# Chunked attention, soft mixture of experts and a softplus MLP on one core: where the 1 MB expert loads stand in SyncE's load queue

## The chip, the cores and the metric

The kernel runs on one core of one Trainium2 chip. The metric is device time in microseconds for one execution; lower is better. All weights and inputs lie in HBM when the kernel starts, and every load is issued by SyncE (SP) on one hardware DMA queue.

## What is computed

Attention is done in chunks of 64 rows inside each head, its output becomes the token matrix x (4608 x 512), a soft mixture of experts turns x into another 4608 x 512 matrix, and an MLP with softplus follows:

```python
scores = scale * np.matmul(q_c, k_c.transpose(0, 1, 2, 4, 3))   # 8 x 8 heads, 9 chunks of 64
attn = softmax(scores); out = np.matmul(attn, v_c)
x = out.transpose(0, 2, 1, 3).reshape(4608, 512)
logits = x @ phi                                  # 32 slots, 8 experts with 4 each
slot_input = softmax(logits, axis=0).T @ x
h = np.maximum(slot_input[e] @ w1[e], 0.0)        # w1: 8 x 512 x 1024
slot_out[e] = h @ w2[e]                           # w2: 8 x 1024 x 512
x = softmax(logits, axis=1) @ slot_out
g = softplus(x @ w_in); out = g @ w_out           # 512 -> 2048 -> 512
```

All of it is float32. w1 and w2 are 16 MiB each.

## The kernel before

The work has three stages on the engines' streams.

**Attention** goes through 36 units, each two heads by 512 tokens. The steps of a unit u are `lq` (loads q and k, 256 KB each, line 265, or 261 for the first four units), `lv` (loads v for two units, line 272), `A0`/`A1` (TensorE transposes of q and k, line 406), `S` (scores, line 437), `C` (transposes of the probabilities, line 470), `D` (times v, line 489), `E` (transposes of x, line 524), and every fourth unit `F` and its followers (the router's logits, lines 542 to 614). q and k have three buffers each, `raw`; unit u+3 can be loaded once `A1` of unit u has run.

**The experts.** The w1 weights come in sixteen loads of 1 MiB, and so do the w2 weights (`load`, lines 285 to 307; a load into a slot w0 to w7 is issued as two DMAs of 512 KB). The list `W1` names the SBUF slot of each w1 load, `W2` that of each w2 load. Slots w, g and i lie beside attention's buffers; the five slots d0 to d4 (loads 5 to 9 of w1) lie in attention's own space. A step `close` gives up attention's buffers piece by piece: d0 needs all `A1`, d1 and d2 need all `S`, d3 and d4 need all `D`. Once attention is done, `H` number n multiplies the slot inputs by w1 load n (line 933, eight matmuls each), and `SO` number n multiplies the hidden values by w2 load n (line 975, sixteen matmuls each). Loads 5 to 15 of w2 go into slots that an `H` or `SO` has to have read before: load 5 (slot w0) follows `H` 0, load 6 follows `H` 1. Beside `SO` runs the chain `c1` to `c6`, `d`, `dc` (lines 795 to 858): the token's softmax over slots, in three groups, each ending in a GpSimd step `c6` (line 845) and three times four TensorE transposes `d` (line 852) into cT. Before `SO` 14 and `SO` 15 stand four and three pairs of filling matmuls (line 916, table `FILL`).

**The MLP** follows: 72 steps of matmuls (lines 1086, 1144, 1146, 1148) with softplus on VectorE, ScalarE and GpSimd.

The order on every engine is made when the program is built: `issue` (lines 74 to 136) is a list scheduler. It takes the steps with their costs (table `COST`, in microseconds), buffers and ranks, simulates one clock for each engine, and at every turn issues the step that can start first, by rank where several can. A step with `after` isn't issued before the steps named there. What it picks is the order in each engine's stream; on the chip each engine goes through its stream in that order. A `lw` step (a 1 MiB load) has a rank of 100 or more, an `lq` step the rank of its unit, so a `lw` step goes between two `lq` steps only where the simulated SP would otherwise stand idle.

Of the kernel before, what the change touches and what calls it, by code (L numbers as in the profile page):

```python
# [17 lines left out]
LAG = 3  # L18
BUSY = 36
WAIT = 0  # L20
FILL = {("SO", 14): 4, ("SO", 15): 3, ("o", 0): 2}


# [8 lines left out]


COST = {
# [110 lines left out]
def kernel(  # L145
# [56 lines left out]
    def open_pool(nm):  # L202
        c = ExitStack()
        pools[nm] = c.enter_context(tc.tile_pool(
            name="slots_" + nm, bufs=1, side="right", reuse_waits="tile"))
        pool_ctx.append(c)
# [411 lines left out]
    by = {}  # L618

    def add(nm, key, fn, deps=(), take=(), give=(), rank=0.0, cost=None, after=()):  # L620
        s = Step(nm, key, fn, [by[d] for d in deps if d in by], take, give, rank, cost,
                 [by[d] for d in after])
        by[nm, key] = s
        steps.append(s)

    for u in range(NU):
# [4 lines left out]
            cost={"SP": 2.4} if G == MIXED else None)  # L631
# [27 lines left out]
        n = HP - 1 if G == NG - 1 else 0  # L659
# [61 lines left out]
    def at(f, *a):  # L721
        return lambda e, held: f(*a)

    for n, sl in enumerate(W1):
        if sl[0] != "d":
            add("lw", ("w1", n), at(load, "w1", n, sl), rank=100 + n)
    for n in range(5):
        add("lw", ("w2", n), at(load, "w2", n, W2[n]), rank=130 + n)
    ends = ((raw_ctx, "A1", ["d0"]), (qk_ctx, "S", ["d1", "d2"]), (v_ctx, "D", ["d3", "d4"]))
    deps = []  # L730
    for i, (c, nm, sls) in enumerate(ends):
        add("close", i, at(lambda c, sls: (c.close(), [open_pool(sl) for sl in sls]), c, sls),
            deps + [(nm, k) for k in range(NU)])
        deps = [("close", i)]
        for sl in sls:
            n = W1.index(sl)
            add("lw", ("w1", n), at(load, "w1", n, sl), deps, rank=110 + n)

    def warm_up(x, n):
        p = tr_tile(0)  # L740
# [11 lines left out]
    for a in range(4):  # L752
        sl = slice(32 * a, 32 * a + 32)
# [3 lines left out]
    for a in range(4):  # L757
        sl = slice(32 * a, 32 * a + 32)
# [155 lines left out]
    def fill(key, t):  # L914
        for _ in range(FILL.get(key, 0)):
            nc.tensor.matmul(
                out=t[:, 0:256], lhsT=ident, rhs=acc[:, 0:256], start=True, stop=True)
# [277 lines left out]
    for nm, n in AFTER:  # L1195
        r += 1
        if nm == "wi":
            for pr in range(2):
                sl = WI[n][0][pr]
# [3 lines left out]
        else:  # L1203
            sl = W2[n] if nm == "w2" else f"w{n}"
# [74 lines left out]
    for c in range(4):  # L1279
# [4 lines left out]
        n, d = need[c]  # L1284
# [21 lines left out]
    for n in range(NQ):  # L1306
        t, qd = order[n]
        ps = pieces.get(n, [(0, 4)])
        b, j = divmod(t // 2, 3)
# [62 lines left out]
    for s in steps:  # L1372
# [12 lines left out]
        if s.nm in ("cb0", "cx0") and s.key[:2] == ("wi", 1):  # L1385
            s.after = [*s.after, by["mx", (WAIT, 0)]]

# [31 lines left out]
```

## Time and profile before

| | |
|---|---|
| Median of 3 runs | 681.0 us (674.77 to 687.27) |
| The profiled execution | 677.68 us |
| its span on the core | 675.9 us |
| mean granted TensorE clock, share of full speed | 0.982 |
| TensorE matmuls busy | 636.2 us (94%) |
| moved by DMA | 107.93 MB |

The profile is that of one execution. The span runs from the first to the last instruction; the profiled execution's own time is 1.8 us longer. Times in the trace count from the start of the span. Attention ends at about 171 us, `H` runs from 174 to 188, `SO` from 192 to 224, and the MLP takes the rest.

### The profile page before, as it was taken

What the parts mean: (1) busy time and instruction counts of PE and PEld (TensorE: products, weight loads), DVE (VectorE), ACT (ScalarE), POOL (GpSimd) and SP (SyncE); (2) the same over time, 40 slices, a digit from 0 to 9 for tenths busy, and PEclk for the clock granted to TensorE, in tenths of its full rate; (3) what the DMA queues carried; (4) which work ended last, traced back from release to release, by engine and by line L of the source; (5) the groups of instructions that cost most, each with busy time, mean ns of one, the idle gap of its engine ahead of it and who ended that gap; (6) DMA issues with size and microseconds to landing.
All of it is one profiled execution on the core that took longest, in us unless ns stands there. A gap on an engine that the chain in (4) does not pass through costs nothing.

```text
span 675.9 us, 14115 instructions
## 1 busy us (share of the span) xinstructions
PE 636.2 (94%) x5849; PEld 511.0 (76%) x5849; DVE 428.0 (63%) x630; ACT 335.0 (50%) x511; POOL 237.9 (35%) x205
## 2 busy tenths in 40 slices
PE   5899889988987899999999999999999999999997
PEld 4688777766354677788788788888888888888885
DVE  1678777775337699879887867754555554545551
ACT  2575556553136699734655955544333333333330
POOL 4233233220214446513222234444433344443341
PEclk7999999999997999999999999999999999999999
DMA  9799879899999803112313410222414222231412
GB/s 176 194 253 267 247 216 289 225 322 419 413 409 410 357 32 112 44 64 93 125 64 123 189 63 31 82 75 79 110 62 126 63 86 101 78 110 64 120 36 62
DMA packets 80543, 107.93 MB, mean 160 GB/s; under 512 B 42464, under 2 KB 60896, under 8 KB 78560
## 3 DMA queue, kind: packets, MB, share of 16 engines
q1 hardware_dynamic: 80480, 107.04, 48.9%
q8 instruction: 46, 0.75, 0.4%
q14 instruction: 17, 0.14, 0.1%
HBM read 88.15 MB, written 18.87 MB: 158 GB/s over the span
## 4 chain that ended last, share of the span: by engine, by line
PE 83%; DVE 7%; ACT 3%; issue 3%; POOL 1%; DMA 1%; SPq 1%; POOLq 0%; DVEq 0%; ACTq 0%
PE trm L1148 18%; PE trm L1146 18%; PE trm L1144 18%; PE ph L1086 5%; PE tr L406 4%; PE X L489 3%; PE S L437 2%; PE tr L470 2%; PE tr L524 2%; PE hps L933 2%; PE sops L975 2%; PE tr L542 2%; PE tr L600 1%; DMA q<-in_q_dram 1%; DVE nm L448 1%
## 5 line engine op out<-in xcount | busy, mean ns | idle before, releaser
L1125 POOL TENSOR_TENSOR g<-hTm,g 128x1024 fp32r<-128x1024 f32 (+1 forms) x37 | 87.3, 2359 | 105.2 <-ACT g L1121 101.4
L1111 ACT ACTIVATE hTm<-hTm 128x1024 f32<-128x1024 f32 (+2 forms) x51 | 51.5, 1011 | 77.6 <-DVE hTm L1105 77.3
L1105 DVE TENSOR_SCALAR hTm<-ph 128x1024 uint32<-128x1024 uint32 (+2 forms) x51 | 59.0, 1157 | 35.8 <-PE ph L1086 35.8
L423 POOL COPY T<-T 64x512 f32<-64x512 f32 x72 | 43.9, 610 | 102.5 <-ACT T L415 101.7
L1115 DVE SCALAR_TENSOR_TENSOR hTm<-ph,hTm 128x1024 f32<-128x1024 f32 (+1 forms) x37 | 44.2, 1194 | 24.8 <-ACT hTm L1111 24.7
L1121 ACT CAST g<-hTm 128x1024 fp32r<-128x1024 f32 (+1 forms) x37 | 38.0, 1026 | 39.6 <-DVE hTm L1115 39.6
L1160 DVE TENSOR_TENSOR i<-trm,i 128x512 f32<-128x512 f32 x52 | 35.7, 686 | 31.6 <-PE trm L1148 31.4
L415 ACT COPY T<-tr 128x512 f32<-128x512 f32 x72 | 40.9, 588 | 25.3 <-PE tr L406 25.2
L1086 PEld LDWEIGHTS ph<-cT,Tc 128*128 128x128 f32 x288 | 43.6, 190 | 11.6 <-issue 3.1
L1086 PE MATMUL ph<-cT,Tc 128*128 128x256 f32 x288 | 47.1, 286 | 2.1 <-DVE ph L1115 1.7
L1105 DVE TENSOR_SCALAR siT<-ph 128x1024 uint32<-128x1024 uint32 (+1 forms) x25 | 29.5, 1180 | 25.8 <-PE ph L1086 25.8
L1111 ACT ACTIVATE siT<-siT 128x1024 f32<-128x1024 f32 (+1 forms) x25 | 25.7, 1028 | 36.9 <-DVE siT L1105 36.9
L1125 POOL TENSOR_TENSOR g<-siT,g 128x1024 fp32r<-128x1024 f32 x12 | 28.9, 2404 | 42.5 <-ACT g L1121 42.5
L1125 DVE TENSOR_TENSOR g<-ph,g 128x1024 fp32r<-128x1024 f32 (+2 forms) x27 | 29.8, 1102 | 11.1 <-ACT g L1121 11.1
L448 DVE TENSOR_REDUCE nm<-S 128x8 f32<-128x512 f32 x36 | 24.7, 687 | 16.7 <-PE S L437 16.6
L1121 ACT CAST g<-ph 128x1024 fp32r<-128x1024 f32 (+2 forms) x27 | 24.9, 921 | 20.6 <-DVE ph L1115 17.0
L406 PE MATMUL tr<-ident,q 128*128 128x128 f32 x144 | 29.1, 285 | 6.1 <-DMA q<-in_q_dram 5.0
L437 PE MATMUL S<-T 64*64 64x64 f32 x1152 | 24.9, 223 | 7.1 <-DVE P L454 2.5
L437 PEld LDWEIGHTS S<-T 64*64 64x64 f32 x1152 | 20.7, 135 | 14.4 <-issue 10.0
L406 PE MATMUL tr<-ident,k 128*128 128x128 f32 x144 | 28.6, 280 | 1.2 <-issue 1.1
L462 ACT ACTIVATE P<-P 128x512 f32<-128x512 f32 x36 | 22.9, 638 | 11.6 <-DVE P L454 11.6
L454 DVE TENSOR_TENSOR P<-S,nm 128x512 f32<-128x512 f32 x36 | 24.5, 680 | 2.1 <-PE S L437 1.3
(457 smaller groups left out, 1770.5 us busy)
## 6 DMA issues: line engine op xcount, KB each, us to landing
part<-i SPq DMA_DIRECT2D x18, 512.0 KB, 2.6
i<-part SPq DMA_DIRECT2D x18, 512.0 KB, 3.6
q<-in_q_dram SPq DMA_DIRECT2D x32, 256.0 KB, 4.2
k<-in_k_dram SPq DMA_DIRECT2D x32, 256.0 KB, 4.6
vbm<-in_v_dram SPq DMA_DIRECT2D x40, 128.0 KB, 4.3
g<-in_moe_w_dram SPq DMA_DIRECT2D x5, 1024.0 KB, 7.9
d<-in_moe_w_dram SPq DMA_DIRECT2D x5, 1024.0 KB, 12.3
i<-in_moe_w_dram SPq DMA_DIRECT2D x5, 1024.0 KB, 15.6
```

The source lines that it names most:

```text
L406: nc.tensor.transpose(c, t[:, h, 2 * rr:2 * rr + 2, :].rearrange("p r d -> p (r d)"), ident)
L423: nc.gpsimd.tensor_copy(out=t[a:a + 64, :, 1], in_=t[b:b + 64, :, 2 * h])
L437: nc.tensor.matmul(out=sp[64 * o:64 * o + 64, b, 64 * i:64 * i + 64], lhsT=cs[:, 0], rhs=cs[:, 1], start=True, stop=True)
L1086: nc.tensor.matmul(out=ph(n, a, b)[:, j - a, :], lhsT=K["Tc"][:, f * 128:(f + 1) * 128], rhs=K["cT"][:, t * TT:(t + 1) * TT], start=True, ...
L1105: nc.vector.tensor_scalar(out=scratch(n, a, b).bitcast(U32), in0=ph(n, a, b).bitcast(U32), scalar1=0x80000000, scalar2=None, op0=ALU.bitwi ...
L1111: nc.scalar.activation(out=y, in_=y, func=AF.Softplus)
L1115: nc.vector.scalar_tensor_tensor(out=soft(n, a, b), in0=ph(n, a, b), scalar=0.0, in1=y, op0=ALU.max, op1=ALU.add)
L1121: nc.scalar.copy(out=V["gs", n][:, 0, a:b], in_=soft(n, a, b))
L1125: tt(e)(out=s[:, 1, a:b], in0=soft(n, a, b), in1=s[:, 0, a:b].bitcast(F32), op=ALU.subtract)
L1144: nc.tensor.matmul(out=po, lhsT=s[:, 0, j, ts_], rhs=wr[:, hs], start=(n in begin and j == 0), stop=False)
L1146: nc.tensor.matmul(out=po, lhsT=s[:, 0, j, ts_], rhs=wr[:, ls], start=False, stop=False)
L1148: nc.tensor.matmul(out=po, lhsT=s[:, 1, j, ts_], rhs=wr[:, hs], start=False, stop=(j == 3 and n in finish))
```

## The change

A new table `PARK` gives seven of the w1 loads a rank that is the number of a unit, instead of 100 and more, and ties each with `after`: load n comes behind the `lq` step before unit PARK[n] and ahead of that of unit PARK[n]. The costs of `lq`, `lv` and of these loads in the scheduler's table are set lower. The five loads into d0 to d4 get a rank of 140 and more and depend on the first five w2 loads.

```diff
+PARK = {0: 9, 1: 14, 2: 18, 3: 22, 4: 26, 10: 30, 11: 33}
 FILL = {("SO", 14): 4, ("SO", 15): 3, ("o", 0): 2}
...
-    "lq": {"SP": 1.7}, "lv": {"SP": 2.7}, "lwi": {"SP": 1.35},
+    "lq": {"SP": 1.55}, "lv": {"SP": 2.45}, "lwi": {"SP": 1.35},
...
     for n, sl in enumerate(W1):
         if sl[0] != "d":
-            add("lw", ("w1", n), at(load, "w1", n, sl), rank=100 + n)
+            add("lw", ("w1", n), at(load, "w1", n, sl), rank=PARK.get(n, 100 + n),
+                cost={"SP": 2.35} if n in PARK else None)
+            if n in PARK:
+                by["lq", PARK[n]].after = [by["lw", ("w1", n)]]
+                by["lw", ("w1", n)].after = [by["lq", PARK[n] - 1]]
...
         for sl in sls:
             n = W1.index(sl)
-            add("lw", ("w1", n), at(load, "w1", n, sl), deps, rank=110 + n)
+            add("lw", ("w1", n), at(load, "w1", n, sl), deps + [
+                ("lw", ("w2", j)) for j in range(5)], rank=140 + n)
```

On SP's queue, five 1 MiB loads stand between attention's q, k and v loads before (slots w0, w1, g0, g1, g2), and nine now: w0, w1, w4, g0, g1, g2, w5, w2, w3 (w4 and w5 have no entry in the table; the scheduler finds them a place). The end of attention's loads reads, before:

```order
L272 DMA vbm_115<-in_v_dram 128x4x64 x4
L265 DMA q_2682<-in_q_dram 128x2x256
L265 DMA k_2683<-in_k_dram 128x2x256
L265 DMA q_2741<-in_q_dram 128x2x256
L265 DMA k_2742<-in_k_dram 128x2x256
L304 DMA g2_2789<-in_moe_w1_dram 128x2048
L265 DMA q_2834<-in_q_dram 128x2x256
L265 DMA k_2835<-in_k_dram 128x2x256
L272 DMA vb2_116<-in_v_dram 128x4x64 x4
```

and with the change, the same stretch of SP's queue, from the 1 MiB load in slot w2 on:

```order
L300 DMA w2a_2440<-in_moe_w1_dram 128x1024
L300 DMA w2b_2441<-in_moe_w1_dram 128x1024
L266 DMA q_2483<-in_q_dram 128x2x256
L266 DMA k_2484<-in_k_dram 128x2x256
L266 DMA q_2513<-in_q_dram 128x2x256
L266 DMA k_2514<-in_k_dram 128x2x256
L273 DMA vbm_115<-in_v_dram 128x4x64 x4
L266 DMA q_2608<-in_q_dram 128x2x256
L266 DMA k_2609<-in_k_dram 128x2x256
L300 DMA w3a_2654<-in_moe_w1_dram 128x1024
L300 DMA w3b_2655<-in_moe_w1_dram 128x1024
```

Two of the loads that stood behind the last v load, slots w2 and w3, stand here now; w4 and w5 stand earlier.

On the same queue behind attention's last v load, before (after the loads into w2 to w6, which stand ahead of g3):

```order
L304 DMA g3_3235<-in_moe_w1_dram 128x2048
L304 DMA d0_3270<-in_moe_w1_dram 128x2048
L304 DMA d1_3287<-in_moe_w1_dram 128x2048
L304 DMA d2_3316<-in_moe_w1_dram 128x2048
L304 DMA d3_3324<-in_moe_w1_dram 128x2048
L304 DMA d4_3326<-in_moe_w1_dram 128x2048
L304 DMA i0_3328<-in_moe_w2_dram 128x2048
L304 DMA i1_3330<-in_moe_w2_dram 128x2048
L304 DMA i2_3332<-in_moe_w2_dram 128x2048
L304 DMA i3_3334<-in_moe_w2_dram 128x2048
L299 DMA w7a_3336<-in_moe_w2_dram 128x1024
L299 DMA w7b_3337<-in_moe_w2_dram 128x1024
```

and now (ahead of g3 stands only the load into w6):

```order
L305 DMA g3_2981<-in_moe_w1_dram 128x2048
L305 DMA i0_3032<-in_moe_w2_dram 128x2048
L305 DMA i1_3132<-in_moe_w2_dram 128x2048
L305 DMA i2_3169<-in_moe_w2_dram 128x2048
L305 DMA i3_3213<-in_moe_w2_dram 128x2048
L300 DMA w7a_3268<-in_moe_w2_dram 128x1024
L300 DMA w7b_3269<-in_moe_w2_dram 128x1024
L305 DMA d0_3297<-in_moe_w1_dram 128x2048
L305 DMA d1_3326<-in_moe_w1_dram 128x2048
L305 DMA d2_3334<-in_moe_w1_dram 128x2048
L305 DMA d3_3336<-in_moe_w1_dram 128x2048
L305 DMA d4_3338<-in_moe_w1_dram 128x2048
```

The five d loads, which wait for attention's steps, have moved behind the first five w2 loads, which wait for none. What follows in the queue, from w2 load 5 on, is in the same sequence in both.

TensorE's stream in the `SO` stage, where `sops` rows are `SO` matmuls (two to a row, two rows to each half of a slot) and `trm` from `cr` are the `d` transposes. Before, from the last transposes of the first group on:

```order
L852 MATMUL trm_3588<-ident,cr 128x128 x4
L975 MATMUL sops_3360<-w1a,hTm 32x256 x2
L975 MATMUL sops_3361<-w1a,hTm 32x256 x2
L975 MATMUL sops_3360<-w1b,hTm 32x256 x2
L975 MATMUL sops_3361<-w1b,hTm 32x256 x2
L852 MATMUL trm_3610<-ident,cr 128x128 x4
L852 MATMUL trm_3623<-ident,cr 128x128 x4
L852 MATMUL trm_3630<-ident,cr 128x128 x4
L975 MATMUL sops_3360<-w2a,hTm 32x256 x2
```

and now, the first three `d` of the stream:

```order
L981 MATMUL sops_3361<-w2b,hTm 32x256 x2
L858 MATMUL trm_3626<-ident,cr 128x128 x4
L981 MATMUL sops_3360<-w3a,hTm 32x256 x2
L981 MATMUL sops_3361<-w3a,hTm 32x256 x2
L981 MATMUL sops_3360<-w3b,hTm 32x256 x2
L981 MATMUL sops_3361<-w3b,hTm 32x256 x2
L858 MATMUL trm_3648<-ident,cr 128x128 x4
L858 MATMUL trm_3653<-ident,cr 128x128 x4
L981 MATMUL sops_3360<-w4a,hTm 32x256 x2
```

The three transposes of the first group stood ahead of `SO` 0 (two) and behind `SO` 5 (one); they now stand behind `SO` 7 (slot w2) and `SO` 8 (slot w3). The last three `d` of the stream now stand behind `SO` 13, just ahead of the filling matmuls of `SO` 14; before, the last one stood behind `SO` 9. In attention the scheduler also interleaves the same transposes and matmuls a little differently from the tenth unit on. From the first MLP step on, the five engines' streams are the same in both.

## Rows read from the trace of the kernel before

**Rows 1.** The page: busy time by engine; the queue that carries instructions.

```profile
PE 636.2 (94%) x5849; PEld 511.0 (76%) x5849; DVE 428.0 (63%) x630; ACT 335.0 (50%) x511; POOL 237.9 (35%) x205
...
q8 instruction: 46, 0.75, 0.4%
```

**Rows 2.** Stretches: us, busy PE, PEld, DVE, ACT, POOL, clock, DMA share, GB/s.

```profile
40.00:60.00 20.00, 19.55 (x482) 15.94 (x484) 17.02 (x38) 13.09 (x28) 7.37 (x13) 1.00 0.91 237
60.00:80.00 20.00, 18.21 (x432) 15.27 (x425) 16.29 (x39) 11.14 (x24) 5.42 (x9) 1.00 0.88 256
80.00:100.00 20.00, 16.73 (x439) 13.89 (x442) 13.72 (x31) 11.19 (x25) 6.17 (x11) 1.00 0.83 234
100.00:120.00 20.00, 18.48 (x454) 15.41 (x446) 16.35 (x37) 13.02 (x27) 5.90 (x10) 1.00 1.02 288
120.00:140.00 20.00, 19.14 (x442) 15.41 (x442) 16.04 (x38) 11.45 (x28) 5.69 (x10) 1.00 0.87 242
...
210.00:223.00 13.00, 13.00 (x121) 8.02 (x120) 8.56 (x11) 7.79 (x12) 6.13 (x4) 0.78 1.02 411
```

**Rows 3.** Chain of waits, 172 to 226 us: start, length, what.

```profile
174.44 13.91 PE hps L933 x128
...
190.77 0.90 PE trm L852 x8
191.68 5.34 PE sops L975 x96
...
209.64 1.97 PE trm L852 x8
...
218.80 1.92 PE hps L916 x8
...
221.90 1.49 PE hps L916 x6
223.39 1.05 PE sops L975 x15
```

**Rows 4.** SP's timeline: start, time in the queue, DMA issued.

```profile
59.23 0.46 SPq L299 DMA_DIRECT2D w0a<-in_moe_w_dram  x1
...
136.61 0.37 SPq L265 DMA_DIRECT2D q<-in_q_dram  x1
...
151.66 12.38 SPq L304 DMA_DIRECT2D d<-in_moe_w_dram  x5
...
170.18 0.33 SPq L299 DMA_DIRECT2D w7b<-in_moe_w_dram  x1
175.46 0.33 SPq L299 DMA_DIRECT2D w0a<-in_moe_w_dram  x1
...
206.88 4.15 SPq L304 DMA_DIRECT2D i<-in_moe_w_dram  x4
```

**Rows 5.** DMA from issue to landing (last number, us), 170 to 224 us.

```profile
i<-in_moe_w_dram SPq DMA_DIRECT2D x4, 512.0 KB, 12.6
...
w7b<-in_moe_w_dram SPq DMA_DIRECT2D x1, 512.0 KB, 17.5
```

**Rows 6.** DMA issues on the page: median us from issue to landing, last number.

```profile
i<-part SPq DMA_DIRECT2D x18, 512.0 KB, 3.6
q<-in_q_dram SPq DMA_DIRECT2D x32, 256.0 KB, 4.2
```

**Rows 7.** Chain of waits, 57 to 66 and 75 to 125 us: start, length, what.

```profile
61.35 1.02 issue
...
119.40 1.12 issue
```

**Rows 8.** What TensorE's weight loads waited for, 20 to 172 us.

```profile
PEld X L489 <- DMA vbm<-in_v_dram: 1.0, 2, 0.8
```

**Rows 9.** TensorE's timeline near attention's last q transposes.

```profile
149.97 0.44 PE L406 MATMUL tr<-ident,q 128*128 128x128 f32 x2
```

**Rows 10.** Groups by line, 172 to 226 us: busy us, mean ns | idle.

```profile
L852 PE MATMUL trm<-ident,cr 128*128 128x128 f32 x36 | 6.6, 337 | 6.0 <-POOL cr L845 6.0
```

## The prediction

> **What bounds the kernel now.** I read the page first: TensorE's matmuls are busy for 94% of the span [rows 1], but that is a mean over three stages. The change doesn't touch the MLP, whose streams are the same, so the question is when the last `SO` ends and how long attention takes. The busy times by stretch answer what fills the two stages. In attention, TensorE is busy for 16.7 to 19.6 of each 20 us, and the DMA engines have a mean share of 0.90 between 40 and 140 us (0.91, 0.88, 0.83, 1.02, 0.87) at 234 to 288 GB/s; from 210 to 223 us the share is 1.02 at 411 GB/s [rows 2]. A share of 1.02 is a full set of DMA engines. So attention leaves about a tenth of the DMA time unused, and it is the share that says so; by GB/s alone it would look like 40%.
>
> Next the chain of waits through the experts: `H` from 174.44 for 13.91 us, six `SO` from 191.68 (96 matmuls, 5.34 us, 0.89 each), then from 209.64 to the end at 223.39 + 1.05 = 224.44 TensorE without a pause [rows 3]. The page of waits would call that TensorE's time; SP's timeline shows what stands just behind it. The last four halves of w2 loads are issued from 206.88 to about 210.7, and they take 12.6 us to land [rows 4, 5], so the last lands at about 223.3, when `SO` 15 starts. The filling matmuls before it (1.92 and 1.49 us) [rows 3] were placed to pass that time. Loads and TensorE end together here: to end sooner, both have to.
>
> **The loads (minus).** Nothing is added or removed; four loads of 1 MiB (slots w2 to w5) go from behind attention's last v load to between its loads. One is 1,048,576 bytes / 411 GB/s = 2.55 us of a full queue [rows 2], so four take 10.2 us from the backlog. In before, the backlog when `H` 0 releases slot w0 ends with w7b: issued 170.18, landed 17.5 us later, 187.7 [rows 4, 5]. Behind it come 14 MiB to the last half of w2 load 15 (w2 loads 5 to 15, two of w_in, one of w_out): 14 x 2.55 = 35.7, which gives 223.4 and so checks the reading. With four loads fewer ahead, the backlog ends at 177.5. There is a floor: w2 load 5 is issued at 175.46, the moment `H` 0 lets it [rows 4], and a 512 KB load on a quiet queue lands after 3.6 us [rows 6], of which 1.3 is its own transfer, so the queue moves again at 177.8. The two agree within 0.3; the queue runs dry for an instant. Last landing 177.8 + 35.7 = 213.5; plus the last `SO` (1.05), 214.5. That is 9.9 us sooner.
>
> **The d loads (nothing).** They wait for attention's steps at the queue's head: SP spends 12.38 us on issuing the five in before [rows 4]. Now w6, g3, the four i and w7, 7 MiB or 17.9 us of transfers, go ahead of that wait, and behind the d loads stand only loads that need an `H` anyway, so nobody is held up. d0's `H` now comes eighth and d4's twelfth of sixteen; 12 x 13.91 / 16 = 10.4 us after 174.44 is 184.9, and the last d, issued in before at about 164 when the last `D` was done [rows 4], has landed by 178. If that cover were gone, TensorE would wait for d0, whose `H` starts 7 x 0.87 after 174.44, at 180.5.
>
> **TensorE through `SO` (a smaller minus).** From the stream as it now stands: `H` ends as before at 188.35, the hidden values are transposed until 190.77 [rows 3], then sixteen `SO` of 0.89 (14.2), nine `d` of 0.45 (8 transposes took 0.90; 4.0) and the filling (3.4) [rows 3]: 212.4 without any wait. In before the `d` waited 6.0 us for the GpSimd step `c6` [rows 10]. The order now puts more `SO` ahead of them, but the chain has its own pace. Bounds: no wait, 212.4, where the loads' 214.5 decides; all 6.0 again, 218.4. I take half, 3.0, since one of the two groups that waited still stands late: 215.4, which is 9.0 us sooner than 224.44. So TensorE decides by a hair. The worse case, half-speed matmuls, is a rival below.
>
> **Attention (plus).** Two prices. First, q, k and v come later when a 1 MiB load stands ahead of them. The last q is issued at 136.61 and transposed at 149.97 [rows 4, 9], 13.4 us later, while a q takes 4.2 us to land [rows 6]; 9 us are to spare, three loads of 2.55. And the only wait of TensorE for a load between 20 and 172 us was 1.0 us for v [rows 8], with five such loads between. The fullest stretch is 40 to 60 us: 0.91 x 20 = 18.2 us of DMA work, plus two loads, 23.3, of 20.4: 2.9 us late, inside the 9. From 100 to 140 it was 37.8, plus two, 42.9 of 40.8: 2.1 late. I take nothing; the bounds are nothing and 10.2, if all four new loads are waited for in full.
>
> Second, the pauses called "issue", in which TensorE waits for nothing that the trace shows. Between 57 and 125 us four of 0.8 us or more (the first 1.02, the last 1.12; two of the four are shown) each follow 2 to 9 us behind a 1 MiB load's issue; the first load goes out at 59.23, the first pause is at 61.35 [rows 4, 7]. With five loads in attention, that is 4 x 1.07 / 5 = 0.86 per load, and four more cost 3.4. Bounds: nothing, and 4 x 1.12 = 4.5. I take 3.4, the rows' own rate.
>
> [...]
>
> **The sum.** 3.4 - 9.0 = -5.6. Startup of the MLP from the last `SO` on moves with it: its w_out loads are in the same sequence and also come ten us sooner. The profiled execution goes from 677.7 to 672.1. The median of the runs shown is 0.5% above that execution, so I put 675.4 for a median.
>
> **Rivals.** (a) Attention pays nothing and TensorE waits little: the loads decide, -9.9, 667.8, as a median 671. For it: TensorE waited for one load in 150 us. Against it: the pauses.
>
> (b) The gain stays on TensorE. [...] Eight `d` transposes then took 1.97 instead of 0.90 [rows 3]. If the stream waits 6.0 again and runs about 4 us slower (three or four `SO` and some `d` at half speed, as in before), it ends at 222.4, and 2.0 sooner less 3.4 is +1.4: 679.1, as a median 682. It speaks against it that eight `SO` in a row now stand ahead of the first `d`, so TensorE is less likely to rest early.
>
> (c) Slower: q and k come late. Attention needs three buffers' lead for this; from the point at which a q lands more than 13.4 us after its issue, each further 1 MiB load is on TensorE's path at its full 2.55. Four cost 10.2, with the pauses 13.6; `SO` starts that much later and keeps only its 9.0: +4.6, 682.3, as a median 686. If the five older ones are exposed too, 12.8 more: 695, as a median 698. For it: from 100 to 120 us the share is 1.02 already. Against it: in that very stretch TensorE was busy for 18.48 of 20 us [rows 2].
>
> (d) The loads are only moved in the queue and the time stays: that would be so if the DMA engines were full throughout. Between 40 and 140 us about 10 us of 100 were free, so it can't be excluded that some of it can't be used; it would show as (b), with 0 to -3.
>
> **How the numbers follow.** My forecast 0.45; (a) 0.22; (b) with (d) 0.21; (c) 0.12, of which half reaches 690 and more. Runs of before spread by 1% around the median, so the range adds some 4 us at each end: from (a)'s 671 down to 667, and from (b)'s 682 and the milder (c) up to 686. A measurement can tell about 2% from no change here; 2% is 667.4 and 694.6. Faster by more than that needs (a) with a lucky run: 0.1. Slower needs the full (c): 0.06. The rest is within.
>
> **What would show it.** Right: the last `SO` ends at 215 to 219, attention (the first `H`) starts at 175 to 179, the DMA share from 40 to 140 us is about 1.0, "issue" pauses in attention are more by 3 us, and w2 load 5 lands within 5 us of its issue (17.5 for the load ahead of it in before). Wrong: waits of TensorE's q or k transposes for DMA (c); a last `SO` beyond 221 with idle TensorE behind `c6` (b); an `H` that waits for a d load; a DMA share in attention that has not risen, so that the loads were not carried there.

## The result and the profile after

The changed kernel takes 689.75 us as a median (684.63 to 692.02), the kernel before 680.56 us beside it: a ratio of 1.0127, with a 95% interval of 1.0078 to 1.0177. It is slower, by less than the 2% that the prediction drew as its line, and outside the range that it gave. The profiled execution has a span of 690.2 us, 14.3 longer than that of before.

The first view is the busy time by stretch of the kernel before, cut at the first `H` and at the end of the last `SO` (columns as in [rows 2]):

```profile
20.00:174.44 154.44, 137.57 (x3178) 113.37 (x3181) 112.22 (x256) 85.31 (x185) 43.71 (x69) 0.99 0.91 276
174.44:224.44 50.00, 43.82 (x452) 22.94 (x452) 23.22 (x39) 22.38 (x36) 13.61 (x9) 0.90 1.02 411
224.44:675.90 451.46, 442.38 (x2084) 364.80 (x2082) 288.58 (x327) 221.84 (x282) 172.88 (x92) 1.00 0.27 91
```

The same three stretches of the changed kernel, which end at other times, and below them five stretches of attention that answer to [rows 2]:

```profile
20.00:192.43 172.43, 144.67 (x3179) 118.29 (x3181) 113.86 (x257) 86.66 (x185) 43.32 (x69) 0.95 0.89 273
192.43:238.35 45.92, 41.08 (x453) 21.36 (x452) 23.25 (x42) 20.65 (x33) 13.65 (x9) 0.96 0.97 378
238.35:690.20 451.85, 443.51 (x2082) 365.86 (x2082) 288.83 (x327) 221.92 (x282) 173.16 (x92) 0.99 0.27 88
...
40.00:60.00 20.00, 15.44 (x326) 13.10 (x328) 11.92 (x26) 9.35 (x19) 4.68 (x9) 0.91 0.82 216
60.00:80.00 20.00, 17.82 (x451) 14.49 (x443) 13.34 (x32) 10.65 (x23) 5.27 (x9) 0.91 0.91 263
80.00:100.00 20.00, 16.73 (x378) 13.39 (x370) 13.91 (x36) 10.94 (x27) 5.25 (x9) 1.00 0.94 288
100.00:120.00 20.00, 18.41 (x448) 15.08 (x441) 16.11 (x35) 12.71 (x27) 6.36 (x11) 1.00 0.91 260
120.00:140.00 20.00, 17.12 (x437) 13.99 (x431) 12.72 (x31) 9.37 (x20) 4.78 (x8) 1.00 0.94 263
```

Attention is 18.0 us longer, the experts' stage 4.1 us shorter, the MLP the same within 0.4. Within attention TensorE has the same instructions (3179 matmuls against 3178) and is busy for 7.1 us more, at a mean granted clock of 0.95 instead of 0.99; the other 10.9 us it is idle. What it was idle for is in the view of TensorE's waits. Before (20 to 174 us; the four rows put down to issue; who waited, what for: us in total, times, longest):

```profile
PE tr L542 <- issue: 3.0, 3, 1.1
PE tr L406 <- issue: 2.1, 2, 1.1
PE S L437 <- issue: 1.9, 1, 1.9
PE X L489 <- issue: 1.6, 3, 0.7
```

and after (20 to 192 us; two more such rows have 0.9 and 0.2):

```profile
PE S L438 <- issue: 10.7, 7, 4.0
PE X L490 <- issue: 5.1, 2, 2.7
```

That is 8.6 us before and 16.9 after, and nearly all of it now stands before scores (`S`) and the product with v (`X`, the step `D`). No row of TensorE's waits in attention names a load of q, k or v. The chain of waits of the changed kernel shows where the longest pauses lie (start, length, what), which answers to [rows 7]:

```profile
42.44 3.98 issue
63.09 2.02 issue
...
148.40 2.68 issue
...
168.41 2.43 issue
```

The longest of before was 1.9 us (the row of `S` above). Lastly the experts' stage, again from the chain, to be laid beside [rows 3]:

```profile
192.43 14.15 PE hps L939 x128
...
209.53 8.82 PE sops L981 x128
...
222.58 1.83 POOL cr L851
...
229.41 2.06 POOL cr L851
...
231.52 1.53 PE trm L858 x12
233.05 1.73 PE hps L922 x8
234.78 1.01 PE sops L981 x16
235.79 1.49 PE hps L922 x6
237.28 1.04 PE sops L981 x16
```

Eight `SO` now run without a break, and then TensorE stands behind the GpSimd step `c6` of the second and the third group. Its waits from 192 to 238 us have this for it, against the 6.0 us of [rows 10]:

```profile
PE trm L858 <- POOL cr L851: 4.1, 2, 2.5
```

### The profile page after: what moved, and what is told of

It is laid out like the page before. It is cut to its first block, busy times and chain, and to the rows that moved or that the text cites. A ratio compares the mean times of both kernels' runs of the same rounds, so it can differ in the third digit from the quotient of the medians.

```text
span 690.2 us, 14090 instructions
## 1 busy us (share of the span) xinstructions
PE 642.2 (93%) x5849; PEld 516.1 (75%) x5849; DVE 429.6 (62%) x633; ACT 334.7 (48%) x508; POOL 238.0 (34%) x205
## 4 chain that ended last, share of the span: by engine, by line
PE 81%; DVE 6%; issue 5%; ACT 3%; POOL 2%; DMA 1%; SPq 1%; POOLq 0%; ACTq 0%; DVEq 0%
PE trm L1154 18%; PE trm L1152 18%; PE trm L1150 18%; PE ph L1092 5%; PE tr L407 4%; PE X L490 3%; PE S L438 3%; PE tr L525 2%; PE tr L471 2%; PE hps L939 2%; PE sops L981 2%; PE tr L601 1%; DVE nm L449 1%; DMA q<-in_q_dram 1%; PE tr L543 1%
## 5 line engine op out<-in xcount | busy, mean ns | idle before, releaser
L1121 DVE SCALAR_TENSOR_TENSOR hTm<-ph,hTm 128x1024 f32<-128x1024 f32 (+1 forms) x37 | 44.2, 1193 | 24.6 <-ACT hTm L1117 24.6
L1092 PEld LDWEIGHTS ph<-cT,Tc 128*128 128x128 f32 x288 | 43.6, 190 | 11.9 <-issue 2.8
L449 DVE TENSOR_REDUCE nm<-S 128x8 f32<-128x512 f32 x36 | 24.6, 684 | 14.5 <-PE S L438 14.3
```

What stands on the lines that cost most here:

```text
L1092: nc.tensor.matmul(out=ph(n, a, b)[:, j - a, :], lhsT=K["Tc"][:, f * 128:(f + 1) * 128], rhs=K["cT"][:, t * TT:(t + 1) * TT], start=True, ...
L1121: nc.vector.scalar_tensor_tensor(out=soft(n, a, b), in0=ph(n, a, b), scalar=0.0, in1=y, op0=ALU.max, op1=ALU.add)
```

## The experiments

Two things changed at once in attention: where the 1 MiB loads stand in SP's queue, and the order in which the scheduler interleaves attention's steps on every engine, since its costs and ranks were changed. Theory L (and, from the second series on, F, which gives it a mechanism) holds the loads responsible, theory O or D the order. In most runs the scheduler decides the order and a second table decides where on SP the loads are put, so that one can be changed without the other. Each line of the table is one kernel's profile; the ratio is that of its timed runs to those of before on the same chip. "Pauses" are TensorE's waits put down to issue between 20 us and the first `H`, summed over the view's rows, "loads" its waits for a DMA there. A row is one execution: the three with before's order and five loads differ by 6.3 us in their first `H`, so a difference of a few us between two rows is not clear of that.

| kernel | order of attention | 1 MiB loads between | first `H` | last `SO` matmul starts | pauses | loads | ratio (interval) |
|---|---|---|---|---|---|---|---|
| before | before | 5 | 174.4 | 224.1 | 8.6 | 0.0 | 1 |
| before_again | before | 5 | 177.4 | 227.3 | 9.0 | 0.6 | one execution |
| d_only | before | 5 | 180.7 | 230.4 | 11.9 | 0.0 | 0.9988 (0.9952 to 1.0024) |
| none | before | 0 | 172.4 | 231.4 | 5.6 | 0.2 | 1.0051 (1.0026 to 1.0076) |
| loads_only | before | 9 | 182.0 | 230.4 | 7.1 | 3.1 | 1.0057 (1.0018 to 1.0096) |
| after | after | 9 | 192.4 | 237.9 | 16.9 | 0.0 | 1.0127 (1.0078 to 1.0177) |
| after_again | after | 9 | 194.1 | 239.4 | 18.1 | 0.2 | one execution |
| order_only | after | 5 | 188.0 | 237.2 | 14.3 | 0.0 | 1.0084 (1.0052 to 1.0116) |
| order_none | after | 0 | 176.3 | 241.7 | 8.4 | 0.0 | 1.0187 (1.0117 to 1.0258) |
| cost_order | lower costs alone | 5 | 187.3 | 234.0 | 10.5 | 1.9 | 1.0125 (1.0046 to 1.0205) |
| park_oldcost | change, old costs | 7 | 182.1 | 230.5 | 7.4 | 2.0 | 1.0064 (1.0030 to 1.0098) |
| spaced | see below | 5 | 174.4 | 225.4 | 5.7 | 1.1 | 0.9959 (0.9929 to 0.9990) |
| spaced_nine | see below | 9 | 190.2 | 238.9 | 12.3 | 5.8 | 1.0126 (1.0049 to 1.0203) |

**loads_only.** All compute engines have word for word the order of before; SP alone has the loads where the changed kernel has them.

```diff
+PLACE = {9: [0], 14: [1], 17: [12], 18: [2], 22: [3], 26: [4], 29: [13], 30: [10], 33: [11]}
...
             V["qk", u] = ts
+            for n in PLACE.get(u, ()):
+                load("w1", n, W1[n])
```

(the step `lw` of these nine then issues nothing)

> The order of every compute engine is word for word that of the kernel before; only SP's queue differs: the nine 1 MiB loads stand before the same units' q loads as in the changed kernel (units 9, 14, 17, 18, 22, 26, 29, 30, 33), the d loads where they were. Theory L (the loads among attention's loads hold TensorE up, without a wait for q, k or v: pauses put down to issue): first H at 185 to 195 us instead of 174, pauses of TensorE put down to issue between 20 us and the first H 14 us or more (8.6 before, 16.9 in the changed kernel), total 685 to 695. Theory O (the changed interleave of attention's steps is slower in itself): first H at 173 to 178, pauses about 9, total 670 to 681.

First `H` at 182.0, pauses 7.1 us, 1.0057. That is between the two theories: slower than before, but not by what the changed kernel lost, and its pauses are no longer than before's. Part of what it lost is something else: 3.1 us of waits of the transposes for q and k, which before hardly had, and matmuls that are busy for 3.7 us more than in before_again (143.2 against 139.6 us).

**order_only.** The reverse: the changed kernel, with `PLACE = {17: [0], 20: [1], 25: [2], 29: [3], 35: [4]}` and the other four loads behind the last v load.

> The order of every compute engine is that of the changed kernel; in SP's queue the 1 MiB loads are back where they stood before: five before units 17, 20, 25, 29 and 35, four behind the last v load; the d loads stay behind the first w2 loads. Theory L: first H at 172 to 179, pauses of TensorE put down to issue 7 to 11 us, total 675 to 684. Theory O: first H at 186 to 195, total 687 to 695.

First `H` at 188.0, pauses 14.3 us, 1.0084. Theory L's numbers fall, theory O's are met. Order alone (+0.84%) and loads alone (+0.57%) add up to 1.41%, and the whole change measured 1.27% (0.78 to 1.77): two causes. The order is the larger by the first `H` (see d_only below), while the intervals of the two ratios overlap. In order_only TensorE also waits 2.1 us for d loads behind the first `H`, which it doesn't in the changed kernel, so its total isn't the price of attention's order alone.

**none.** The kernel before, with all nine loads behind the last v load.

> The kernel before with no 1 MiB load among attention's loads: all nine stand behind the last v load. Theory L: pauses fall below 5 us, first H at 166 to 172; the backlog is 12.8 us longer, so the last SO ends at about 232 to 237 and the total is 683 to 693, set by the loads. Theory O: pauses and first H as before (8.6 us and 174 us), last SO at 236, total 687 to 693.

First `H` at 172.4 with 5.6 us of pauses (theory L had 166 to 172 and below 5), total 0.5% slower, because the `SO` now wait for a longer backlog (the last `SO` matmul starts at 231.4). With before's order, 0, 5 and 9 loads between give a first `H` at 172.4, 177.5 (the mean of three profiles) and 182.0: each load of 2.55 us costs attention about 1 us, with one profile each at 0 and at 9 loads.

**d_only.** Only the last hunk of the change's diff, the d loads behind the first w2 loads.

> The kernel before with only the d loads moved behind the first five w2 loads (rank and dependency as in the change). Attention's order is that of before, five 1 MiB loads between. Both theories: first H at 173 to 176 as before. The loads' backlog at the first H is the same, so the last SO ends at 221 to 225 and the total is within 3 us of before.

The total is unchanged (0.9988). Its first `H` at 180.7 was expected at 173 to 176, and with it the last `SO` ended at 230.8 instead of 221 to 225: attention's streams and loads are those of before, so this is the spread of one kernel between executions, and the profile of before was a short one. Compared with the mean of 177.5, the changed kernel's two profiles (192.4 and 194.1) lose 15.8 us in attention, not 18.0; order_only loses 10.5 and loads_only 4.5 of it.

**dense.** Why would an order of the same matmuls cause pauses? The scores and the product with v are series of small matmuls, 16 of them to a step in the program and 32 in the trace, each with its own weight load, in about 0.65 us. This kernel puts the same stretch of such matmuls in twice.

```diff
+    def dense(ts):
+        for i in range(640):
+            h, b = i % 2, i // 2 % 2
+            o = h ^ b
+            nc.tensor.matmul(
+                out=ts[b][64 * o:64 * o + 64, 0:64], lhsT=ident[64 * h:64 * h + 64, 64 * h:64 * h + 64],
+                rhs=ident[64 * h:64 * h + 64, 64 * h:64 * h + 64], start=True, stop=True)
```

> The kernel before with the same stretch of 640 extra small matmuls (64x64 by 64, each with its own weight load, results overwritten) put in twice: behind the last H, where the DMA engines are full (share 1.02), and in the MLP ahead of step 60, where their share is about 0.26. Theory F (TensorE's instructions arrive through the DMA engines; dense series of small matmuls outrun them, the more so the fuller the DMA engines): the first stretch has pauses put down to issue of 5 us or more in all and takes at least 5 us longer than the second. Rival P (pauses belong to the small matmuls themselves): both stretches take the same time within 2 us. Rival N (no such pauses in a long series): both run at about 0.02 us for a matmul, 13 us, without a pause over 0.5 us.

The chain of waits in the first stretch, behind the last `H` (start, length, what):

```profile
192.95 3.60 issue
196.56 3.02 PE sops L931 x128
199.58 3.17 issue
202.75 3.69 PE sops L931 x68
206.44 2.51 issue
208.95 3.69 PE sops L931 x128
...
215.14 3.31 PE sops L931 x128
218.46 0.14 issue
218.60 2.10 PE sops L931 x128
```

and in the second, in the MLP:

```profile
636.75 1.14 issue
637.88 2.09 PE ph L931 x128
639.97 1.65 issue
641.63 2.09 PE ph L931 x128
```

Between two pauses stand 128 matmuls and their 128 weight loads (the row with x68 lacks records), over and over, in both stretches. The view of the DMA over the second stretch (634 to 668 us) has this for the queue that carries instructions (packets, MB, share of 16 engines):

```profile
q8 instruction: 10, 0.16, 2.2%
```

Ten packets of 16 KB (0.16 MB) for 2560 instructions: one for each 256. The author read the pauses from this as TensorE waiting for the next packet, that is, for its next block of 256 instructions. How long one lasted went with the other traffic. The busy time by stretch of this kernel (last two numbers: DMA share, GB/s):

```profile
190.20:212.00 21.80, 12.52 (x546) 12.00 (x545) 0.42 (x1) 0.37 (x1) 0.00 (x0) 0.67 1.01 404
...
220.00:234.00 14.00, 8.01 (x500) 7.46 (x496) 0.00 (x0) 0.00 (x0) 0.00 (x0) 1.00 0.01 4
634.00:668.30 34.30, 21.10 (x1282) 19.75 (x1281) 0.20 (x1) 0.00 (x0) 1.99 (x1) 1.00 0.04 12
```

With the DMA engines full (share 1.01), a block took 6.2 us from start to start (196.56, 202.75, 208.95); with them quiet (0.04), 3.4 to 3.8 us in the second stretch. The first stretch took about 10 us longer than the second (44.2 against 34.1), though loads filled only its first half: 4.6 us of that are longer pauses, 5.2 us longer busy time. The clock isn't what stretches a block: the one that starts at 215.14 still runs slowly (3.31 us, mean granted clock 0.63 from 212 to 220 us), but the loads are over (DMA share 0.09 in the same 8 us), and the next block starts 3.46 us later, as in the quiet stretch. Theory F is met, and the rivals P and N fall; that pauses of 1.4 us remain with quiet DMA engines belongs to P and was not in F's numbers.

That attention's pauses are the same thing is a reading too; the DMA packets of the traces speak for it. The DMA view of the changed kernel's longest pause (42.44 to 46.42 us) has one packet on this queue:

```profile
q8 instruction: 1, 0.02, 1.8%
```

In the thirteen profiles of the table TensorE has 89 pauses of 0.3 us or more put down to issue between 20 us and the first `H`. Each of them ends 1.1 to 1.6 us after a packet of this queue has landed (the nine in before 1.25 to 1.57, the eight in the changed kernel 1.27 to 1.59); a moment taken at random in the changed kernel's attention lies that far behind a packet in 8% of cases. The queue sends 25 packets from 20 us to the first `H` both in before and in the changed kernel, so the new order doesn't need more packets; its pauses are longer (16.9 us against 8.6 in all).

Behind the long pauses the granted clock was lower as well: in the dense kernel the same 128 matmuls take 3.69 us instead of 2.09 (mean granted clock 0.67 from 190.2 to 212 us, 1.00 from 634 to 668.3). In the changed kernel the mean granted clock is 0.50, 0.65, 0.60 and 0.50 behind its four longest pauses (46.42 to 49.42, 65.11 to 70.00, 151.08 to 155.30 and 172.40 to 175.80 us). That is much of the second part of what attention lost, its 7.1 us of longer busy time.

The MLP's matmuls are longer: in before TensorE is busy for 442.38 us with 2084 of them, 0.21 us each, and has no wait put down to issue from 225 us on.

**order_none.** The changed kernel's order with none of the nine loads between.

> Compute engines in the order of the changed kernel; no 1 MiB load among attention's loads, all nine behind the last v load. Against the run with the order of before and none between (first H 172.4). Theory F: with the DMA engines less full the new order loses most of its handicap, first H at 173 to 180, pauses of TensorE put down to issue 5 to 9 us. Rival D (the new order is slower by its waits between steps, whatever the loads): first H at 182 to 188. Total 688 to 697 in both, since the backlog of loads ends later.

First `H` at 176.3. The two rows of TensorE's waits put down to issue, 20 to 176 us:

```profile
PE S L443 <- issue: 3.8, 4, 2.3
PE X L495 <- issue: 3.4, 2, 2.4
```

With all such rows, 8.4 us. Theory F is met, and rival D, which had the first `H` at 182 to 188, is not: the same order that is 10.5 us behind with five loads between, and about 11 with nine (193.3 against 182.0), is 3.9 us behind without any (176.3 against 172.4). So most of what the order costs comes with the traffic beside it; the sizes rest on one profile each.

Its total, 1.0187, is the longest in the table for another reason. With the whole backlog behind attention, the d loads, which the change puts behind the first w2 loads, come last, and `H` stands behind them (TensorE's waits, 176 to 242 us):

```profile
PE hps L950 <- DMA d<-in_moe_w_dram: 15.5, 4, 12.8
```

In none, where the d loads stand ahead of the w2 loads, the same wait is 0.9 us.

**cost_order.** Only the two lower costs of `lq` and `lv`, the loads held where they were before.

```diff
-    "lq": {"SP": 1.7}, "lv": {"SP": 2.7}, "lwi": {"SP": 1.35},
+    "lq": {"SP": 1.55}, "lv": {"SP": 2.45}, "lwi": {"SP": 1.35},
```

> The kernel before with only the two lower costs of lq and lv in the scheduler's table (1.55 and 2.45); the 1 MiB loads are put before the same units as in the kernel before, so that the order of attention's steps is what differs. It has series of S, D and F of 5 steps, as the changed kernel does. Theory F and theory D both: slower than before if those series are what costs: first H at 182 to 190, total 684 to 692. If the numbers in the cost table are harmless and PARK made the order bad: first H at 174 to 181, total within 3 us of before.

First `H` at 187.3, 1.0125. These numbers cost nothing on the chip by themselves; they make the scheduler run ahead with the transposes of q and k and put series such as D, S, F, S, D behind each other. But pauses are only 10.5 us here: of the 9.9 us against before_again, 1.5 are pauses, 1.3 waits for loads and 3.6 longer busy time; the rest are waits of steps for each other. So the pauses are not all of what makes an order bad; how they share it with plain waits between steps, beyond these two kernels, stays open.

**park_oldcost.** The whole change without those two numbers (seven loads come between).

> The whole change but for the two costs of lq and lv, which stay at 1.7 and 2.7. The scheduler then puts seven 1 MiB loads between attention's loads and makes another order. If the lower costs made attention's order bad (as the run with the costs alone says), this is faster than the changed kernel: first H at 178 to 186, total 680 to 687. If PARK spoils the order as much by itself: first H at 187 to 193, total 687 to 692.

First `H` at 182.1, 1.0064: half of the loss is gone, as expected.

**spaced and spaced_nine.** A rule in the scheduler: a third step of small matmuls in a row is put back.

```diff
+                if e == "PE" and s.nm in DENSE and run >= 2:
+                    t += 0.3
...
+            run = run + 1 if s.nm in DENSE else 0
...
+DENSE = {"S", "D", "F"}
```

> The kernel before, with a rule in the scheduler: a step of small matmuls (S, D, F) that would be the third such step in a row starts 0.3 us later in its simulation, so others go first. Series of S, D and F of 3 or more steps: 5 instead of 9, none of 4 or more. The 1 MiB loads stand before the same units as in the kernel before. Theory F: pauses of TensorE put down to issue at or below those of before (8.6 and 11.9 us in two profiles), first H at 172 to 178, total 674 to 681. Rival D (what counts is how steps wait for each other): no relation, first H anywhere from 174 to 190.

> Compute engines in the order of the run with the scheduler's rule against long series of small matmuls; nine 1 MiB loads between attention's loads, before the same units as in the changed kernel; the d loads as before. Theory F (instructions reach TensorE through the DMA engines): the loads cost about as much as they did in the order of before, first H 3 to 10 us behind the 174.4 of the same order with five loads, total 683 to 690, not faster than with five. Rival: once long series are gone there is room for the loads, first H at 172 to 177, and the last SO ends 4 us sooner than with five, total 674 to 680.

With five loads it is the fastest kernel of the study, 0.9959 (0.9929 to 0.9990), with 5.7 us of pauses: 0.4% below before. Its first `H` at 174.4 is no earlier than that of before's shortest profile, so the rule's gain in attention isn't clear of the spread. With nine loads the same order loses 15.8 us of attention, more than F's 3 to 10, so F's number was missed here. TensorE's waits there (20 to 190 us):

```profile
PE X L499 <- issue: 8.2, 4, 2.6
PE S L447 <- issue: 3.9, 3, 2.8
PE tr L416 <- DMA k<-in_k_dram: 3.5, 4, 1.7
PE tr L416 <- DMA q<-in_q_dram: 2.3, 3, 1.0
```

5.8 us are waits for q and k, the rival (c) of the prediction, which in the changed kernel itself didn't occur. Fewer long series don't make room for the loads.

**before_again and after_again.** The two kernels once more.

> The kernel before once more, for the spread of attention's length between executions: first H between 174 and 182, since two profiles with its attention stream and the same five loads gave 174.4 and 180.7; pauses of TensorE put down to issue 8 to 13 us.

> The changed kernel once more, for the same spread: first H between 186 and 194 (192.4 in its first profile), pauses put down to issue 13 to 18 us, last SO 44 to 48 us behind the first H.

The first as expected (177.4 and 9.0), the second a hair above two of its bounds (194.1, 18.1 and 45.3 from the first `H` to the start of the last `SO` matmul).

## Why the prediction was wrong, by its own steps

**Attention.** The step that failed is "Two prices": there were three. The one that the prediction left out is the order of attention's steps, which its front part only called "a little differently" interleaved. It is worth 10.5 us with five loads between (188.0 against 177.5), and the cost numbers alone bring 9.9. The two prices that it did name came out near their size in sum, 3.4 forecast and 4.5 measured in loads_only, but that is luck: they were split wrongly there, since pauses didn't rise (7.1 us), while waits for q and k (3.1 us) and busy time (3.7 us) did. The nothing that it took for late q and k holds in the changed kernel and not in loads_only.

**The pauses' cause.** They were read as something that follows a 1 MiB load. The rows allowed that, but it is half of it: in the dense kernel a pause came after every 256 instructions, 1.1 to 1.7 us long with quiet DMA engines and 2.5 to 3.6 us with full ones. The rate was also taken low: it divides four pauses by five loads, while the fifth load goes out at 133.73 us, behind the stretch that was read, and all of attention has 8.6 us of pauses. What was missing was the question which stretches of the stream use up instructions fastest, and whether the change moves them.

**The loads.** The floor was read rightly: w2 load 5 goes out 1.3 us behind the first `H` in the changed kernel (1.0 before), and the queue does run dry there. It is dry for more than the instant that was forecast: the DMA share is 0.59 from 192.43 to 198 us. SP's timeline after, to be laid beside [rows 4]:

```profile
193.69 0.33 SPq L300 DMA_DIRECT2D w0a<-in_moe_w_dram  x1
...
217.88 4.14 SPq L305 DMA_DIRECT2D i<-in_moe_w_dram  x4
```

and from issue to landing, 192 to 238 us ([rows 5] before):

```profile
i<-in_moe_w_dram SPq DMA_DIRECT2D x4, 512.0 KB, 12.8
...
w0a<-in_moe_w_dram SPq DMA_DIRECT2D x1, 512.0 KB, 4.5
```

w2 load 5 lands after 4.5 us, as said (within 5), and the last load at about 222.0 + 12.8 = 234.8, ahead of the start of `SO` 15 at 237.28. That is 42.4 us behind the first `H`, where the prediction's sum has 39.1 (213.5 less 174.44), so the loads too gained less than forecast. TensorE ends later than they do, as forecast.

**TensorE through `SO`.** The term was mis-sized: from the first `H` to the last `SO`'s end 41.0 us were forecast, 45.9 came, 50.0 were before; so 4.1 us gained instead of 9.0. Of the 4.9 us that are missing, 1.1 are the waits for `c6`: the order that puts eight `SO` ahead of the first `d` was taken to halve them to 3.0, and they are 4.1. Another 0.8 come before the first `SO` (17.1 us behind the first `H` instead of 16.3), and 1.7 in the first eight `SO`: all sixteen were priced at the 0.89 us of the six that ran at a granted clock of 1.00 before, and these eight take 8.82 us at a mean clock of 0.81. The rest is spread over what follows, where an `SO` takes 1.01 to 1.04 us. The chain shows where the waits now stand: behind the second `d` of the stream the second group's copy, `c6` and `d` come one after the other, and the third group's `c6` ends at 231.47, with 6.9 us of `d`, filling and `SO` behind it. That is rival (b)'s place, at a smaller price than it named: the granted clock there is 1.00 from 222 to 238 us, while in before the eight transposes from 209.64 us, on which its half speed rests, ran at 0.50.

**The d loads** cost nothing in the changed kernel, as said: no row of TensorE's waits there names one, and d_only is at 0.9988. With no loads among attention's they do cost, as order_none shows. **The MLP** moved with the last `SO` as said (451.46 and 451.85 us).

**The range** ended at 686. Rival (c), the only one well on the slow side, was priced for another mechanism, late q and k; the slowdown came without them. Of the signs of being wrong two appeared: a last `SO` beyond 221 with TensorE idle behind `c6`, and a DMA share in attention that has not risen (0.90 from 40 to 140 us in both kernels, 251 and 258 GB/s). The four loads were carried there all the same; attention, and with it its own loads, went more slowly.

## What to carry to other kernels

A number in a list scheduler's table is an edit of every engine's stream, also where it only names the cost of a load: lay the two orders side by side on the engine that bounds the stage and give the difference a price of its own, or hold the order fixed and move the loads alone. A stretch in which the DMA engines had a tenth of their time free (a share of 0.90 from 40 to 140 us) was not free for other loads here: each 1 MiB load of 2.55 us put among attention's loads cost it about 1 us in the order of before, and packets of instructions came through the same engines beside them, 25 in the 154 us from 20 us to the first `H`. And before a profile is compared with another, take the same kernel's profile twice: attention's length varied by 6 us between executions.

## What was not expected of the hardware

In the dense kernel TensorE paused after every 256 instructions of a series of small matmuls. In a stretch with quiet DMA engines and a granted clock of 1.00 the pauses were 1.1 to 1.7 us, behind full DMA engines 2.5 to 3.6 us; a block of 256 took 3.4 to 3.8 us in the first case and 6.2 in the second, whereas its 128 matmuls alone took 2.09. After the long pauses the matmuls ran slower (3.69 us for the same 128), in a stretch whose mean granted clock was 0.67.
